# New planned durations and a new model of transfers in a list scheduler that orders every engine's stream

## Chip, cores and metric

One NeuronCore of a Trainium2 chip runs the whole program. The metric is device microseconds from launch to end, as the median of several runs. TensorE is called PE in the profile, VectorE DVE, ScalarE ACT, GpSimd POOL; SyncE (SP) issues the transfers. All times here are in us unless marked ns.

## What is computed

Attention that keeps the 32 largest scores of each row, and behind it two feed-forward networks (FFNs) on the same 2304 tokens:

```
scores = scale * q @ k.T                       # 4 batches, 8 heads, 576 positions, 64 wide
kth    = partition(scores, -32)[..., -32]      # the 32nd largest of each row
attn   = softmax(where(scores >= kth, scores, -1e9))
x      = (attn @ v) as (2304 tokens, 512)
h      = x @ w_in;  g = max(0.01 * h, h);  y = g @ w_out               # 512 -> 2048 -> 512
z      = max(y @ w1, y @ w2, y @ w3) @ w_out2                          # 512 -> 768 -> 512
```

The FFNs' weights come as 64-bit floats. The results must be close to 32-bit precision, so a matrix product is made of three 16-bit ones (high part by high, high by low, low by high).

## The kernel before

**Attention** runs in 72 steps, numbered from 0 in the order of the program; a step is 128 query rows of one pair of heads, or 64 rows of two pairs. A step's work goes through all engines in turn:

- SP loads K (`kt`) and Q (`qt`, L397 to L408) from the prepared copy `dqk` in memory; PE multiplies them (L693) into the score tile `s`, of which there is one; ACT copies it to `S` (L698), twice for each step (halves 0 and 1 of `S`; there are three buffers `S`).
- DVE searches the 32 largest: four times `MAX8` (L708) and three times a replace (L710: `MATCH_VALUE_LOAD`, then `MATCH_REPLACE8`) for each half.
- POOL makes the biases `nt` and `nb` (L718 to L727); ACT masks (L732), takes the exponential (L735) and rounds to 16 bits (L738, `phl`); POOL subtracts for the low part (L740).
- SP transposes `phl` to `pt` (L743), PE multiplies with V (L769 to L771, called the weighting product here), DVE takes the reciprocal of the sums (L776, L777), ACT scales (L779) and rounds (L785), POOL subtracts (L787), and once a block is full SP transposes it to `xu` (L805), the input of the FFN.

**Preparation.** For each batch and pair of heads `prep_qk` loads Q and K into `raw` (two buffers; for batch 0 into space of `wo`), squares them (L340), finds a power of two (L325 on DVE, L332 and L334 on POOL), scales (L351), splits (L352, L353) and writes both parts to `dqk` (L380). `v_stats` (L426) and `prep_v` (L440) do the like for V, with the same buffers `raw`. The FFN's weights are repacked from 64 bits by DVE (L487, L490, L493), their norms taken (ACT L512, PE L518, DVE L523), and scaled and split as above (`w<-in_w_in` at L476 and so on).

**The FFNs** run in ten units of 128 to 256 tokens. PE's work in them is groups of three products (L811, L812, L813). Between them stand ACT (L859, L866), POOL (L872) and DVE (L956), and at the change from the first network to the second a chain through L909, L912 and L914. Results go to memory at L994.

**The order.** Nothing of the order is written by hand. Each call of `op` makes a node with its engine, a planned duration, what it reads and writes, and a priority: `TP(i)` for step `i`, less 100 for scores and weighting product, and a running clock for the FFN units. `Plan.run` (L123) is a list scheduler. It goes through planned time; on each engine it takes, of the nodes that may start, the one of lowest priority value, adds the planned duration, and frees buffers at the planned ends. For SP's transfers it keeps one planned path. The planned start times, sorted, give the order in which the instructions are written, and so each engine's fixed order on the chip. On the chip an engine waits for the semaphores of its next instruction and does nothing else meanwhile; planned times themselves appear nowhere in the program.

## Time and profile before

| | us |
|---|---|
| median of 3 runs (1081.46, 1085.2, 1085.3) | 1085.2 |
| the profiled execution, in all | 1083.86 |
| its span, first to last instruction | 1081.9 |
| PE busy | 901.3 |
| DVE busy | 876.3 |
| ACT busy | 840.9 |
| POOL busy | 600.0 |
| mean granted clock of PE, as a share of 2.4 GHz | 0.935 |

The 2.0 us between span and whole lie outside of what the trace shows. Shares over the whole span say little here, since the program has stages: first weights and attention alone, then attention and FFN side by side, at the end the FFN alone. So the profile is read by stage, and where two engines hand work to each other, by the two instructions concerned. A busy time on PE is not PE at its peak, because products overlap.

### The profile page before, as it was taken

The numbers are of one execution on the slowest core, as the hardware profiler recorded it, in microseconds if no ns is written. First come the engines' busy times: TensorE is split into PE (matmuls) and PEld (weight loads), VectorE is DVE, ScalarE is ACT, GpSimd is POOL, SyncE is SP. The second block draws the span as 40 slices with busy tenths as digits, with TensorE's granted clock in tenths as the row PEclk, the third lists the DMA queues.
The fourth block names the chain that finished last, engine by engine and source line by source line (L and its number), as shares of the span: only waits on it lengthen the run. The fifth ranks groups of instructions, "written<-read, shape, count | busy, mean of one in ns | idle before, by whom it ended". The sixth has DMA issues, their size and how long they took to land.

```text
span 1081.9 us, 27366 instructions
## 1 busy us (share of the span) xinstructions
PE 901.3 (83%) x10292; PEld 794.4 (73%) x10292; DVE 876.3 (81%) x2010; ACT 840.9 (78%) x1769; POOL 600.0 (55%) x1110
## 2 busy tenths in 40 slices
PE   2334334498998998998999899999989999999998
PEld 2122223387998887887888688878878897889998
DVE  3999999998999999999649899989599999910101
ACT  7866888898799888788979777888997788664242
POOL 4554766686467655566655545666774555443131
PEclk9995556689999999999999999999999999999999
DMA  7878628647555333354753333554834433220000
GB/s 258 284 195 259 222 52 227 199 102 150 105 124 118 91 80 87 77 125 128 177 127 85 81 70 96 135 122 105 186 83 87 92 72 84 64 56 7 21 2 16
DMA packets 268516, 125.78 MB, mean 116 GB/s; under 512 B 237408, under 2 KB 255328, under 8 KB 266336
## 3 DMA queue, kind: packets, MB, share of 16 engines
q1 hardware_dynamic: 268384, 124.04, 45.7%
q8 instruction: 81, 1.33, 0.5%
q14 instruction: 51, 0.42, 0.1%
HBM read 62.65 MB, written 14.16 MB: 71 GB/s over the span
## 4 chain that ended last, share of the span: by engine, by line
PE 49%; DVE 19%; DMA 11%; ACT 10%; POOL 5%; issue 4%; SPq 2%; POOLq 0%; ACTq 0%; DVEq 0%
PE h L811 8%; PE h L812 8%; PE h L813 8%; DMA pt<-phl 6%; DVE m L708 5%; PE acc L811 5%; PE acc L812 5%; PE acc L813 5%; DVE w L710 5%; PE s L693 4%; DVE acc L487 2%; PE h L769 2%; POOL phl L740 2%; DVE w L493 2%; PE h L770 2%
## 5 line engine op out<-in xcount | busy, mean ns | idle before, releaser
L708 DVE MAX8 m<-w 128x8 f32<-128x576 f32 x432 | 309.1, 747 | 0.2
L740 POOL TENSOR_TENSOR phl<-pp,phl 128x576 f16<-128x576 f32 x144 | 183.8, 1281 | 110.2 <-ACT phl L738 105.4
L872 POOL TENSOR_TENSOR f16t<-k,f16t 128x256 f16<-128x256 f32 (+2 forms) x220 | 136.7, 623 | 190.0 <-ACT f16t L866 165.6
L710 DVE MATCH_REPLACE8 w<-m,w 128x576 f32<-128x576 f32 x288 | 212.2, 742 | 0.0
L811 PE MATMUL h<-k,w 128*128 128x256 f16 (+2 forms) x720 | 187.2, 264 | 9.4 <-ACT k L912 4.8
L812 PE MATMUL h<-k,w 128*128 128x256 f16 (+2 forms) x720 | 187.2, 264 | 4.4 <-POOL k L914 4.1
L813 PE MATMUL h<-k,w 128*128 128x256 f16 (+2 forms) x720 | 187.4, 265 | 0.0
L812 PE MATMUL acc<-f16t,wo 128*128 128x256 f16 (+2 forms) x640 | 165.7, 263 | 3.6 <-POOL f16t L872 3.6
L811 PE MATMUL acc<-f16t,wo 128*128 128x256 f16 (+2 forms) x640 | 165.8, 263 | 0.4 <-ACT f16t L866 0.4
L813 PE MATMUL acc<-f16t,wo 128*128 128x256 f16 (+2 forms) x640 | 165.7, 263 | 0.0
L811 PE MATMUL h<-xu,wi 128*128 128x256 f16 (+1 forms) x576 | 154.5, 268 | 1.3 <-DVE colt L325 0.8
L812 PE MATMUL h<-xu,wi 128*128 128x256 f16 (+1 forms) x576 | 154.5, 268 | 0.0
L813 PE MATMUL h<-xu,wi 128*128 128x256 f16 (+1 forms) x576 | 154.5, 268 | 0.0
L693 PE MATMUL s<-kt,qt 128*128 128x288 f16 (+5 forms) x800 | 107.8, 283 | 50.3 <-ACT S L698 35.8
L866 ACT ACTIVATE f16t<-k 128x256 f16<-128x256 f32 (+2 forms) x220 | 86.1, 393 | 54.2 <-DVE k L956 51.7
L735 ACT ACTIVATE pp<-pp,nb,colt 128x576 f32<-128x576 f32 x144 | 123.1, 862 | 0.2
L708 DVE MAX8 m<-S 128x8 f32<-128x576 f32 x144 | 103.1, 744 | 19.5 <-ACT S L698 19.3
L732 ACT ACTIVATE pp<-S,nt 128x576 f32<-128x576 f32 x144 | 107.8, 768 | 13.0 <-POOL phl L740 8.6
L859 ACT ACTIVATE k<-h,colt 128x256 f32<-128x256 f32 (+2 forms) x160 | 72.0, 452 | 58.5 <-PE h L813 57.5
L693 PEld LDWEIGHTS <-qt 128*128 128x128 f16 (+1 forms) x800 | 62.8, 107 | 68.9 <-issue 43.8
L812 PEld LDWEIGHTS <-w 128*128 128x128 f16 x960 | 94.3, 98 | 19.6 <-issue 11.0
L698 ACT ACTIVATE S<-s 128x576 f32<-128x576 f32 x144 | 92.6, 643 | 18.6 <-PE s L693 17.7
(132 smaller groups left out, 2520.4 us busy)
## 6 DMA issues: line engine op xcount, KB each, us to landing
rw<-in_w SPq DMA_DIRECT2D x18, 512.0 KB, 4.8
w<-in_w_in SPq DMA_DIRECT2D x8, 1024.0 KB, 8.1
w<-in_w_out SPq DMA_DIRECT2D x8, 1024.0 KB, 5.0
raw<-in_qk SPq DMA_DIRECT2D x24, 288.0 KB, 3.3
dqk<-hl SPq DMA_DIRECT2D x48, 144.0 KB, 2.5
kt<-dqk SPq DMA_DIRECT2D x16, 288.0 KB, 3.1
qt<-dqk SPq DMA_DIRECT2D x144, 32.0 KB, 2.2
raw<-in_v SPq DMA_DIRECT2D x12, 352.0 KB, 3.3
```

The source lines that it names most:

```text
L693: T.matmul(p()[osl, h, o:o + w], q()[:, hh, st, :n], k()[:, hh, kc:kc + w], start=st == 0, stop=st == 1, skip_group_check=True)
L698: op(ACT, act(S, True), lambda t=t, p=p: A.activation(t().rearrange("p (a s) -> p a s", a=2), p()[:, :, :288], AF.Copy), r=[p], w=[(Sp, j) ...
L708: op(DVE, dve(S) * 1.03, lambda mc=mc, src=src: V.max(mc(), src()), r=rd, w=[(m, j, 0, r)], pr=pd)
L710: op(DVE, dve(S) * 1.03 + 0.06, lambda mc=mc, src=src, j=j: V.match_replace(out=wp()[:, j], in_to_replace=mc(), in_values=src(), imm_value ...
L732: op(ACT, act(S, aps=1), lambda j=j: A.activation(pp()[:, j], Sb[j](), AF.Prelu, bias=nt()[:, j:j + 1], alpha=STEEP), r=[(Sp, j), nt], w=[ ...
L735: op(ACT, act(S, aps=2), lambda j=j, es=es: A.activation(pp()[:, j], pp()[:, j], AF.Exp, bias=nb()[:, j:j + 1], scale=es), r=[(nb, j), ((" ...
L740: op(POOL, pool(S), lambda j=j: G.tensor_tensor(phl()[:, 1, j], pp()[:, j], phl()[:, 0, j], op=ALU.subtract), r=[(pp, j), (phl, 0, j)], w= ...
L811: T.matmul(out, wt(0), xt(0), start=first, stop=False, skip_group_check=True)
L812: T.matmul(out, wt(0), xt(1), start=False, stop=False, skip_group_check=True)
L813: T.matmul(out, wt(1), xt(0), start=False, stop=last, skip_group_check=True)
L866: op(ACT, act(N), lambda: A.activation(hl()[:, 0, :N], g()[:, 0, :N], AF.Copy), r=[(g, 0)], w=[(hl, 0)], pr=pr)
L872: op(POOL, pool(N) + 0.044, lambda: G.tensor_tensor(hl()[:, 1, :N], g()[:, 0, :N], hl()[:, 0, :N], op=ALU.subtract), r=[(g, 0), (hl, 0)], ...
```

## The change

The planned durations of ACT, POOL, DVE's top-k and three transfers change, and the planner's model of transfers does: before, each transfer held the one path for its whole planned time `n.dma`; now it holds it for 0.6 of that, lands after its whole time, and no transfer may be issued before the eighth last one has landed. No instruction, tile or buffer changes.

```diff
+DSH = 0.6
         dma_free = 0.0
+        lanes = [0.0] * 8
...
-                    t, ok = max(n.ready, t0), True
+                    t, ok = max(n.ready, t0, lanes[-8] if e == SP else 0.0), True
...
             if n.eng == SP:
                 st = max(t + 1.1, dma_free)
-                dma_free = st + n.dma
-                end = dma_free + 0.95
+                dma_free = st + DSH * n.dma
+                end = st + n.dma + 0.95
+                lanes.append(end)
...
 def act(n, psum=False, aps=0):
-    return (n * 0.833 + (70 if psum else 120) + 105 * aps) / 1000
+    return (n * 0.833 + (52 if psum else 94) + 93 * aps) / 1000
...
 def pool(n):
-    return (n * 2.13 + 110) / 1000
+    return (n * 1.905 + 142) / 1000
...
-                    op(DVE, dve(S) * 1.03, lambda mc=mc, src=src: V.max(mc(), src()), r=rd, w=[(m, j, 0, r)], pr=pd)
+                    op(DVE, dve(S), lambda mc=mc, src=src: V.max(mc(), src()), r=rd, w=[(m, j, 0, r)], pr=pd)
...
-                    op(DVE, dve(S) * 1.03 + 0.06, lambda mc=mc, src=src, j=j: V.match_replace(
+                    op(DVE, dve(S) + 0.06, lambda mc=mc, src=src, j=j: V.match_replace(
...
-        op(SP, 2.4, lambda: Y.dma_start_transpose(pt().rearrange("p a c q -> p (a c) q"),
+        op(SP, 2.05, lambda: Y.dma_start_transpose(pt().rearrange("p a c q -> p (a c) q"),
...
-            op(PE, 15 * mm(64) * (1 if full else 2) * (COLD if i < NCOLD else 1), avm, r=[pt] + [(vt, x) for x in range(3)], w=[avb, (xs, "a"), (xhl, "a", i)], pr=pa)
+            op(PE, 15 * mm(68) * (1 if full else 2) * (COLD if i < NCOLD else 1), avm, r=[pt] + [(vt, x) for x in range(3)], w=[avb, (xs, "a"), (xhl, "a", i)], pr=pa)
...
-                op(SP, 1.5, lambda u=u, uo=uo, so=so, w=w: Y.dma_start_transpose(
+                op(SP, 1.25, lambda u=u, uo=uo, so=so, w=w: Y.dma_start_transpose(
```

Besides, POOL's `nt` and `nb` are planned 0.05 to 0.1 shorter, and four terms of 0.044 or 0.06 that were added to `pool(n)` are gone. `dma(nbytes)` stays at 255 GB/s, and the latencies between engines stay. In the changed file a line after L126 has a number higher by up to 3 (L698 is L701 there).

What moves is the order on all five engines; after the first instructions hardly a stretch is the same. Three places follow.

**ACT, at the start.** `S` is the score copy of step 0, `s` its product, `w_76` the first weights of `w_in`, `wo` is batch 0's Q and K, `raw` batch 1's. Before, from the 19th instruction on:

```order
L340 ACTIVATE junk_244,colt<-raw_141 128x576
L352 ACTIVATE wo<-wo 128x576
L512 ACTIVATE junk_254<-w_76 128x512
L352 ACTIVATE wo<-wo 128x576
L351 ACTIVATE w_76<-w_76,colt 128x1024
L352 ACTIVATE wo<-wo 128x576 x2
L352 ACTIVATE wi<-w_76 128x4x256
L512 ACTIVATE junk_280<-w_76 128x512
L698 ACTIVATE S_293<-s_283 128x576
```

Now, from the same place on:

```order
L515 ACTIVATE junk_229<-w_76 128x512
L354 ACTIVATE wo<-wo,colt 128x576
L515 ACTIVATE junk_242<-w_76 128x512
L355 ACTIVATE wo<-wo 128x576
L701 ACTIVATE S_263<-s_245 128x576
L354 ACTIVATE wo<-wo,colt 128x576
L515 ACTIVATE junk_280<-w_76 128x512
L355 ACTIVATE wo<-wo 128x576
L701 ACTIVATE S_263<-s_272 128x576
L354 ACTIVATE w_76<-w_76,colt 128x1024
```

The copy went ahead of the scaling of the first weights and of batch 1's square.

**ACT, at step 33**, where batch 2's preparation falls: `pp` and `phl` are the step's weights, `f16t`, `k` and `acc` are of the FFN unit 3, `hl` and `raw` of batch 2. Before:

```order
L732 ACTIVATE pp_7713<-S_7206,nt_7661 128x576
L866 ACTIVATE f16t_7728<-k_1154_7690 128x256
L351 ACTIVATE raw_7131<-raw_7131,colt 128x576
L351 ACTIVATE raw_7268<-raw_7268,colt 128x576
L352 ACTIVATE hl_7754<-raw_7131 128x576
L859 ACTIVATE k_1161_7764<-h_7720,colt 128x256
L732 ACTIVATE pp_7713<-S_7206,nt_7661 128x576
L866 ACTIVATE f16t_7779<-k_1161_7764 128x256
L698 ACTIVATE S_7799<-s_7663 128x576
L735 ACTIVATE pp_7713<-pp_7713,nb_7673,colt 128x576 x2
L909 ACTIVATE k_1167_7838<-acc_6951,colt 128x256 x2
```

(the step's two `phl` follow twelve and fourteen rows after the last `L735`). Now:

```order
L735 ACTIVATE pp_7612<-S_7100,nt_7604 128x576 x2
L869 ACTIVATE f16t_7633<-k_1141_7597 128x256
L701 ACTIVATE S_7639<-s_7558 128x576
L862 ACTIVATE k_1150_7645<-h_7620,colt 128x256
L738 ACTIVATE pp_7612<-pp_7612,nb_7607,colt 128x576 x2
L869 ACTIVATE f16t_7697<-k_1150_7645 128x256
L741 ACTIVATE phl_7699<-pp_7612 128x576 x2
```

Here the step's six operations stand together, ahead of batch 2's preparation and of the change of networks; beside them stand the 12th and 13th tiles of the FFN unit (of 16) where before there were the 15th and 16th. Counted on PE, 795 groups of three FFN products stand ahead of this step's weighting product, where 829 did.

**SP, where batch 2's last pair of heads is loaded** (`kt`, `qt` out of `dqk_3`), which step 37 waits for. Before:

```order
L380 DMA dqk_3_90<-hl_8575 64x2x576 x2
L440 DMA raw_8643<-in_v 128x704
L743 DMA_TRANSPOSE pt_8652<-phl_8541 128x18x128
L994 DMA out_T<-k_1279_8667 128x256 x2
L994 DMA out_T<-k_1280_8678 128x256 x2
L805 DMA_TRANSPOSE xu_8729<-xhl_8311 128x8x64
L405 DMA qt_8754<-dqk_3_90 128x2x64
```

Now:

```order
L383 DMA dqk_3_90<-hl_8591 64x2x576 x2
L443 DMA raw_8642<-in_v 128x704
L443 DMA raw_8693<-in_v 128x704
L408 DMA qt_8696<-dqk_3_90 128x2x64
L411 DMA qt_8696<-dqk_3_90 64x2x64 x2
L997 DMA out_T<-k_1285_8705 128x256 x2
```

The load of Q passed two transposes and the output stores, and a further load of V came ahead of it.

## Rows read from the trace of the kernel before

**Rows 1.** By stage: length, PE, PEld, DVE, ACT, POOL, clock, DMA share, GB/s.

```profile
30.00:200.00 170.00, 67.31 (x628) 47.66 (x626) 169.92 (x366) 134.71 (x223) 99.42 (x147) 0.67 0.69 210
200.00:320.00 120.00, 102.49 (x1360) 97.01 (x1359) 112.30 (x271) 106.98 (x251) 76.29 (x150) 0.90 0.57 129
320.00:520.00 200.00, 187.30 (x2295) 165.68 (x2292) 194.83 (x454) 172.73 (x376) 122.22 (x232) 1.00 0.44 103
...
960.00:1081.00 121.00, 116.12 (x1263) 108.90 (x1260) 11.78 (x31) 43.00 (x114) 31.73 (x61) 1.00 0.05 15
```

**Rows 2.** Timeline: start, length, instruction; last searches and weighting products of three steps.

```profile
438.87 0.76 DVE L708 MAX8 m<-w 128x8 f32<-128x576 f32 x1
452.80 0.19 PE L769 MATMUL h<-vt,pt 128*128 128x65 f16 x1
...
671.44 0.74 DVE L708 MAX8 m<-w 128x8 f32<-128x576 f32 x1
688.61 0.19 PE L769 MATMUL h<-vt,pt 128*128 128x65 f16 x1
...
925.81 1.41 DVE L708 MAX8 m<-w 128x8 f32<-128x576 f32 x2
938.83 0.19 PE L769 MATMUL h<-vt,pt 128*128 128x65 f16 x1
```

**Rows 3.** Timeline of DVE: searches and replaces without a pause between them.

```profile
34.45 1.41 DVE L708 MAX8 m<-w 128x8 f32<-128x576 f32 x2
35.78 0.07 DVE L710 MATCH_VALUE_LOAD w<-m,w 128x8 f32 x1
...
36.50 0.08 DVE L710 MATCH_VALUE_LOAD w<-m,w 128x8 f32 x1
```

**Rows 4.** DVE where step 0 begins (brackets: idle before, ended by).

```profile
29.69 0.42 DVE L523 TENSOR_REDUCE colt<-h 128x1 f32<-128x256 f32 x1 [5.15 <-PE h L518]
30.03 0.75 DVE L708 MAX8 m<-S 128x8 f32<-128x576 f32 x1
```

**Rows 5.** Timelines of PE and ACT before step 0's score copy.

```profile
25.22 1.17 PE L693 MATMUL s<-kt,qt 128*128 128x288 f16 x4
...
25.27 1.13 ACT L351 ACTIVATE w<-w,colt 128x1024 f32<-128x1024 f32 x1
...
27.46 1.04 ACT L352 ACTIVATE wi<-w 128x1024 f16<-128x1024 f32 x1
28.40 0.61 ACT L512 ACTIVATE junk<-w 128x512 bf16<-128x512 f32 x1
28.92 0.62 ACT L698 ACTIVATE S<-s 128x576 f32<-128x576 f32 x1
```

**Rows 6.** Timeline of SP's issues at the start.

```profile
10.01 1.08 SPq L369 DMA_DIRECT2D raw<-in_qk  x2
```

**Rows 7.** Timeline of PE: first FFN product, and the pace of its groups.

```profile
196.75 0.36 PE L811 MATMUL h<-xu,wi 128*128 128x192 f16 x1
...
452.14 0.27 PE L811 MATMUL h<-xu,wi 128*128 128x256 f16 x1
...
452.47 0.27 PE L811 MATMUL h<-xu,wi 128*128 128x256 f16 x1
```

**Rows 8.** Timelines of SP and DVE where step 37's second half begins.

```profile
544.69 1.24 SPq L380 DMA_DIRECT2D dqk<-hl  x2
...
553.88 0.57 SPq L405 DMA_DIRECT2D qt<-dqk  x1
...
558.69 0.76 DVE L708 MAX8 m<-S 128x8 f32<-128x576 f32 x1 [12.21 <-ACT S L698]
```

**Rows 9.** Waits of PE from 320 to 1050: total, times, longest.

```profile
PE s L693 <- ACT S L698: 7.8, 7, 2.8
PE h L769 <- DMA pt<-phl: 5.0, 8, 1.1
```

**Rows 10.** All 72 transposes of the weights, issue to landing.

```profile
DMA to landing us min/median/max: 3.9/4.0/7.3
```

More of the change, by code (lines that the diff above doesn't have):

```diff
@@ L717, in attention @@
         c2 = lambda c: m()[:, :, c:c + 1].rearrange("p a o -> p (a o)")
-        op(POOL, 0.3, lambda: G.tensor_scalar(nt(), c2(TOPK - 1), -1.0, None, op0=ALU.mult),
+        op(POOL, 0.2, lambda: G.tensor_scalar(nt(), c2(TOPK - 1), -1.0, None, op0=ALU.mult),
            r=tk(0) + tk(1), w=[nt], pr=pr)
-        op(POOL, 0.25, lambda: G.tensor_tensor(nb(), c2(TOPK - 1), c2(0), op=ALU.subtract),
+        op(POOL, 0.2, lambda: G.tensor_tensor(nb(), c2(TOPK - 1), c2(0), op=ALU.subtract),
            r=tk(0) + tk(1) + [(m, 0, 0, 0), (m, 1, 0, 0)], w=[(nb, 0), (nb, 1)], pr=pr)
         if full:
-            op(POOL, 0.34, lambda: G.tensor_scalar(nb(), nb(), ES[b, hps[0]], LNPS, op0=ALU.mult, op1=ALU.add),
+            op(POOL, 0.28, lambda: G.tensor_scalar(nb(), nb(), ES[b, hps[0]], LNPS, op0=ALU.mult, op1=ALU.add),
                r=[(("es", b, hps[0]), 1)], w=[(nb, 0), (nb, 1)], pr=pr)
@@ L726, in attention @@
             for j in range(2):
-                op(POOL, 0.34, lambda j=j: G.tensor_scalar(nb()[:, j:j + 1], nb()[:, j:j + 1], ES[b, hps[j]], LNPS,
+                op(POOL, 0.28, lambda j=j: G.tensor_scalar(nb()[:, j:j + 1], nb()[:, j:j + 1], ES[b, hps[j]], LNPS,
                                                            op0=ALU.mult, op1=ALU.add),
@@ L786, in attention @@
            w=[(xhl, 0, g0)], pr=pr)
-        op(POOL, pool(64 * nh) + 0.06, lambda: G.tensor_tensor(xo(1), xi(), xo(0), op=ALU.subtract),
+        op(POOL, pool(64 * nh), lambda: G.tensor_tensor(xo(1), xi(), xo(0), op=ALU.subtract),
            r=[(xs, h) for h in range(nh)] + [(xhl, 0, g0)], w=[(xhl, 1, g0)], pr=pr)
@@ L871, in hilo @@
                 return hl
-            op(POOL, pool(N) + 0.044, lambda: G.tensor_tensor(hl()[:, 1, :N], g()[:, 0, :N], hl()[:, 0, :N],
+            op(POOL, pool(N), lambda: G.tensor_tensor(hl()[:, 1, :N], g()[:, 0, :N], hl()[:, 0, :N],
                                                      op=ALU.subtract), r=[(g, 0), (hl, 0)], w=[(hl, 1)], pr=pr)
@@ L913, in ffn @@
                r=[(ff, e)], w=[(yh, e)], pr=pr)
-            op(POOL, pool(N) + 0.044, lambda e=e, f=f: G.tensor_tensor(yl()[:, e, :N], f(), yh()[:, e, :N],
+            op(POOL, pool(N), lambda e=e, f=f: G.tensor_tensor(yl()[:, e, :N], f(), yh()[:, e, :N],
                                                               op=ALU.subtract), r=[(ff, e), (yh, e)], w=[(yl, e)],
```

## The prediction

> **What bounds the kernel now.** I read the busy times by stage first, then the start of each engine's stream, then pairs of instructions in which one engine hands a step to the next, and last the waits.
>
> By stage [rows 1]: from 30 to 200 us VectorE works 169.9 of 170 us and TensorE 67 of 170, at a granted clock of 0.67. From 320 to 520 both are nearly full (VectorE 194.8, TensorE 187.3 of 200). After 960 VectorE is done and TensorE alone runs out the last FFN units, 116 of 121 us. So two engines bound this kernel in turn: VectorE (weight repacking and the top-32) until the first FFN unit runs, then the two together, then TensorE. TensorE's work does not change, so the end moves by what TensorE loses or saves in idle time: by how much earlier its FFN work begins, and by how often it must wait for a step of attention that VectorE has not finished.
>
> Each step ends in a weighting product (L769 to L771). Its shortest way from the last top-k search is seen at step 69: the search ends at 925.81 + 1.41 = 927.2, the product starts at 938.83, 11.6 us [rows 2]. At step 28 the same way takes 13.2 us (439.6 to 452.80), at step 47 16.4 us (672.2 to 688.61). So at step 28 TensorE comes only 1.6 us, and at step 47 4.8 us, after the earliest moment at which VectorE lets it.
>
> **The change, part by part.**
>
> *Prices in the planner.* No instruction is added or taken away; a planned duration is only a number. The old prices stood above the trace: a top-k search was planned at 0.689 us and takes 0.665 (two in 1.33), a replace at 0.749 and takes 0.72 [rows 3]; now 0.669 and 0.729. ScalarE and GpSimd come down alike, TensorE's prices were right and stay. So the old plan gave TensorE more FFN work per step than VectorE's real pace needs, which is cover: TensorE arrives late and seldom waits. The new plan takes the cover away. Whatever happens comes from the order.
>
> *The start.* VectorE idles 5.15 us before 29.69 and begins step 0's search at 30.03 [rows 4]. The step's score copy ran at 28.92 on ScalarE, though its product was over at 25.22 + 1.17 = 26.4 [rows 5]: weight scaling stood before it, an operation at 25.27 (1.13 us long, of which some 0.1 overlaps the next), one of 0.94 (27.46 to 28.40) and one of 0.52 (28.40 to 28.92). In the new order 22 instead of 29 ScalarE instructions stand before the copy: away are these three, one more of 0.52, one of about 0.7 and two of about 0.6, in all 4.4 us. If the product came no earlier, the copy could move by 2.5 us only; but K and Q of step 0 also move up in SP's queue, past two loads of a later batch (1.08 us of issue at 10.01) and three writes [rows 6]. Bounds -2.5 and -4.4, taken -4: VectorE's saturated stretch begins 4 us earlier. The work of batch 1 that made room (its first head pair) goes behind step 5, where ScalarE and GpSimd have it to do besides the first FFN unit; no one needs it before step 18.
>
> *The first FFN unit.* It starts at 196.75 [rows 7] and waits for step 5. On VectorE 306 instead of 316 instructions stand ahead of that step's reciprocal: six searches (0.665) and three replaces (0.72) fewer and one repacking operation (0.6) more, 5.6 us less; with the earlier start -9.6 us for TensorE's FFN work. Bounds: 0 if ScalarE, which has 13 instructions fewer there too, holds it up, and -10.
>
> *Does TensorE keep it?* VectorE's own order past step 8 is the same to about 1 us at each step. Its pace is therefore the old one, moved by the start (-4) and by what of its 7.7 us of idle time between 200 and 320 [rows 1] goes; it waits there for TensorE, which now comes earlier: between 0 and -7.7, taken -3. So VectorE runs at -7. Before the weighting product of step 28 stand 18 groups of three FFN products fewer than before (664 for 682), at 0.33 us each (452.14 to 452.47) [rows 7] 5.9 us less cover. The product can start at -7 - 1.6 = -8.6; for the same FFN work TensorE is then at -8.6 + 5.9 = -2.7. Of the 9.6 us won it has stood idle through 7.
>
> *Batch 2.* VectorE waits 12.21 us for step 37's second score copy (558.69) [rows 8]. Its Q load was issued at 553.88, behind four output stores and an x transpose. In the new order stores and transpose stand elsewhere, but a third V load stands ahead of it, which needs a free input buffer. The score parts were written by 545.9, so the load could go about 6 us earlier; with what the preparation itself gains or loses (its VectorE steps stand 4 to 7 us later in a stream that runs 7 earlier) the restart moves by -10 to +1, taken -7.
>
> *Steps 37 to 53.* Here the new order places least FFN work: 34 groups fewer before step 47 (1178 for 1212), 11.2 us. The product can start at -7 - 4.8 = -11.8, so TensorE stands at -11.8 + 11.2 = -0.6 for the same work: nearly all is lost. At step 69 the two orders agree again (1788 and 1787 groups), and what follows is TensorE's alone.
>
> *Other waits.* From 320 to 1050 TensorE waited 7.8 us for score copies and 5.0 for transposed weights [rows 9]. Truer prices could take them away or, with less cover, double them: -8 to +13, taken -1.5.
>
> *Transfers.* The new plan lets each transfer hold the path for 0.6 of its time, so 255 GB/s become 425. In the trace the path moved 210 GB/s while its engines were busy 0.69 of the time (30 to 200 us) [rows 1], some 304 GB/s at full share: the truth lies between the two plans. A transpose of the weights takes 3.9 to 7.3 us to land, median 4.0 [rows 10]; alone it is planned at 4.15. So only those that stand beside other transfers land later than planned. The Trainium skill (DMA: Bandwidth & Descriptors, Rules for kernel authors and Issuing engines are not separate DMA queues) says that DMAs in flight together run on the same 16 engines and only interleave, which speaks against planning 0.6; the trace agrees in part, 304 for 425 GB/s. By that rule every such landing would come late and the slower rival below would be the case.
>
> **The sum.** -0.6 - 1.5 = -2.1 us on the profiled execution's span of 1081.9 us, 1079.8, and with the 2.0 us outside of it (1083.86 in all) 1081.8. The median of the three runs lies 1.3 us above the profiled one, less than the runs differ among themselves; I say 1082.
>
> **Rivals.** *The early start is kept* (faster): if VectorE restarts at step 37 by 12 us or more earlier, or runs at -10 already by step 28, the product of step 47 is no limit and TensorE keeps its -9.6: 1083.9 - 9.6 = 1074; with half of the 12.8 us of waits gone too, 1068. For it: VectorE waited for TensorE in 200 to 320, and the order of step 33 on ScalarE no longer lets the next batch's preparation stand within the step. Against it: batch 2's own chain on VectorE is later in the stream.
>
> *Batch 2 is late* (slower): the place is the Q load of step 37. If the third V load waits for its buffer, or the preparation (4 to 7 us later in the stream) sets the pace, VectorE restarts at 0 or later. TensorE has then 11.2 us less to do before step 47 and the product may start at -4.8: +6.4, and with the same at batch 3 (whose third head pair stands 11 us later in VectorE's stream against a shift of 7) up to +10: 1090 to 1094. It decides from a restart of about -1 on. Transposes that land later than planned add to this, at 0.3 us for each of some 26 steps that lost cover, 8 us if none is hidden.
>
> *Nothing moves*: both orders are paced by VectorE and the FFN's end alike; 1084. This lies within the forecast's own band.
>
> **How the numbers follow.** Forecast (within about 4 us of 1082) 0.42, with nothing moves in it; early start kept 0.36; batch 2 late 0.22. A measurement can tell about 0.5%, 5.4 us, from no change: faster 0.36, same 0.42, slower 0.22. The range leaves out a tenth on either side: down to 1070, between the two prices of the faster rival, up to 1093, near the upper price of the slower one.
>
> **What would show it.** Step 0's search should start at 25 to 27.5 us and the first FFN product at 186 to 190; if they don't, the first two steps are wrong. TensorE should show waits for transposed weights about steps 26 to 29 and 44 to 47 that it did not have; if it has none there, the gain was kept and the time is near 1074. VectorE's restart at step 37 should lie near 552; near 558 or later means the slower rival. The forecast is wrong if the waits of the FFN's own chain (ScalarE and GpSimd to TensorE) grow or vanish by more than some 5 us, since I took them as nearly unchanged.

## The result

The changed kernel takes 1099.8 us (median of 1100.82, 1098.78, 1095.24 and 1101.26) where the kernel before takes 1085.25 beside it: a ratio of 1.0134, 95% interval 1.0095 to 1.0173. It is slower by some 14.5 us, outside the range of the prediction (1070 to 1093). The profiled execution took 1100.82 us, of which the span is 1098.7 (1083.86 and 1081.9 before); the two traces differ by 16.7 us of span. Line numbers of the kernel after are up to three higher (L708 is now L711, L769 is L772, L811 is L814).

By stage, as in [rows 1] (length, PE, PEld, DVE, ACT, POOL, granted clock, DMA share, GB/s), the kernel after:

```profile
30.00:200.00 170.00, 65.62 (x610) 47.01 (x609) 160.43 (x343) 132.67 (x219) 93.84 (x140) 0.65 0.66 203
200.00:320.00 120.00, 99.52 (x1245) 92.83 (x1243) 108.54 (x262) 103.84 (x240) 73.77 (x142) 0.88 0.54 127
320.00:520.00 200.00, 182.43 (x2234) 161.34 (x2231) 187.46 (x435) 161.94 (x355) 114.85 (x216) 0.97 0.45 92
...
978.00:1098.00 120.00, 114.77 (x1249) 107.65 (x1246) 11.77 (x30) 41.99 (x111) 30.93 (x60) 1.00 0.04 11
```

VectorE has lost its full stretch: 160.4 of 170 us where it was 169.9, and it stays lower in the next two stages. TensorE does 5 us less between 320 and 520. The last stage is alike.

**The start.** VectorE where step 0 begins, and the first FFN product, which answer to [rows 4] and [rows 7]:

```profile
23.12 0.42 DVE L526 TENSOR_REDUCE colt<-h 128x1 f32<-128x256 f32 x1 [1.44 <-PE h L521]
...
23.90 0.76 DVE L711 MAX8 m<-S 128x8 f32<-128x576 f32 x1 [0.17 <-ACT S L701]
...
190.07 0.34 PE L814 MATMUL h<-xu,wi 128*128 128x192 f16 x1 [2.29 <-DMA xu<-xhl]
```

The search starts 6.1 us earlier (23.90 for 30.03) and the first FFN product 6.7 (190.07 for 196.75). Both are gone soon after: TensorE begins FFN group 100 (of 2240) 3.8 us later than before and group 400 10.7 later. What VectorE waited for between 40 and 240 us (total, times, longest), in the kernel after:

```profile
DVE colt L534 <- PE h L314: 3.3, 2, 2.7
DVE colt L526 <- PE h L521: 3.2, 3, 2.1
DVE h L490 <- DMA rw<-in_w: 3.2, 6, 1.3
DVE r L779 <- PE h L774: 2.0, 3, 0.9
DVE colt L433 <- PE h L314: 1.3, 1, 1.3
```

and in the kernel before:

```profile
DVE colt L531 <- PE h L311: 1.5, 1, 1.5
DVE colt L325 <- PE h L311: 0.2, 1, 0.2
```

13.0 us against 1.7: for TensorE's sums of squares and weighting products, and for weights still on their way.

**The steps.** Last searches and weighting products of steps 28, 47 and 69, against [rows 2]:

```profile
449.93 1.41 DVE L711 MAX8 m<-w 128x8 f32<-128x576 f32 x2
465.60 0.20 PE L772 MATMUL h<-vt,pt 128*128 128x65 f16 x1 [0.70 <-DMA pt<-phl]
...
683.97 1.41 DVE L711 MAX8 m<-w 128x8 f32<-128x576 f32 x2
698.89 0.19 PE L772 MATMUL h<-vt,pt 128*128 128x65 f16 x1
...
943.42 0.75 DVE L711 MAX8 m<-w 128x8 f32<-128x576 f32 x1
955.53 0.19 PE L772 MATMUL h<-vt,pt 128*128 128x65 f16 x1
```

The products come 12.8, 10.3 and 16.7 us later than before. TensorE's waits for transposed weights in steps 19 to 35, the kernel after (320 to 540 us), then the kernel before (310 to 515 us):

```profile
PE h L772 <- DMA pt<-phl: 4.7, 6, 1.1
```

```profile
PE h L769 <- DMA pt<-phl: 0.7, 3, 0.4
```

So there the cover is missing, as the prediction had it: at steps 27 to 31 TensorE stands before a weighting product for 0.5 to 1.0 us each time.

**TensorE's own pace.** From its first FFN product to the end of the span, with the columns of [rows 1], the kernel before, then the kernel after:

```profile
196.75:1081.93 885.18, 828.29 (x9676) 743.55 (x9674) 698.75 (x1626) 685.63 (x1510) 487.89 (x910) 0.98 0.41 94
```

```profile
190.07:1098.67 908.60, 842.17 (x9690) 753.42 (x9690) 707.52 (x1649) 689.79 (x1524) 492.72 (x918) 0.97 0.42 93
```

This stretch is 23.4 us longer after. TensorE's idle time makes 9.5 us of that (66.4 for 56.9), and its busy time 13.9, though it does the same products. They follow each other more slowly where the granted clock is at its lower level. In the kernel after TensorE waits three times between 331.5 and 335.1 us, for 1.2, 0.5 and 0.9 us; behind that the record gives 0.50 (1.2 GHz) between 335.6 and 340.9, and 1.00 (2.4 GHz) between 341.2 and 346. A group of three products of 128 columns takes 0.32 us in the first stretch and 0.16 in the second (from one L814 to the next):

```profile
336.06 0.31 PE L814 MATMUL h<-k,w 128*128 128x128 f16 x1
...
336.38 0.31 PE L814 MATMUL h<-k,w 128*128 128x128 f16 x1
...
344.98 0.22 PE L814 MATMUL h<-k,w 128*128 128x128 f16 x1
...
345.14 0.22 PE L814 MATMUL h<-k,w 128*128 128x128 f16 x1
```

By the record TensorE has 44 us of its work after the first FFN product at the lower level, where it had 23 before. At half the pace that is some 11 of the 13.9 us, an estimate from these rows. No run changes the clock alone, so what it is worth in the end is not shown.

**The restarts.** Batch 2's last pair of heads (step 37) and batch 3's third (step 56), in the kernel after. The products `h<-colt,ones` are `prep_qk`'s sums of squares on TensorE, from which the scaling, the store of `dqk`, the loads of K and Q and the scores follow:

```profile
560.40 0.28 PE L314 MATMUL h<-colt,ones 128*128 128x1 f32 x2
...
570.91 0.38 SPq L408 DMA_DIRECT2D qt<-dqk  x1
...
576.09 0.76 DVE L711 MAX8 m<-S 128x8 f32<-128x576 f32 x1 [6.66 <-ACT S L701]
...
766.13 0.50 PE L314 MATMUL h<-colt,ones 128*128 128x1 f32 x4
...
780.84 0.16 DVE L328 TENSOR_SCALAR colt<-h 128x1 int32<-128x1 int32 x1 [10.44 <-PE h L314]
787.95 0.16 DVE L328 TENSOR_SCALAR colt<-h 128x1 int32<-128x1 int32 x1 [6.95 <-PE h L314]
791.15 0.76 DVE L711 MAX8 m<-S 128x8 f32<-128x576 f32 x1 [3.05 <-ACT S L701]
```

Before, the same pair of events for step 56:

```profile
745.51 0.95 PE L311 MATMUL h<-colt,ones 128*128 128x1 f32 x8
...
770.97 0.76 DVE L708 MAX8 m<-S 128x8 f32<-128x576 f32 x1 [2.43 <-ACT S L698]
```

Step 37's second half restarts at 576.09 for 558.69 [rows 8], 17.4 later; step 56 at 791.15 for 770.97, 20.2 later. The search of step 56 follows its sum of squares by 25.0 us after and by 25.5 before. And that sum stands, on TensorE, at one place of the FFN's work: behind group 1340 in both orders; the sums of batch 2's second pair stand behind group 780 in both (those of the third and fourth pair behind 826 to 870). Why they stand there: a preparation has the due time of its step less `LB` = 60 and the priority number that follows from it; FFN units with lower numbers go first, whenever their inputs are there. (The sums of batch 2's second pair have the number 364.4; FFN group 779 has 363.5 and group 780 has 364.7.) So VectorE's next batch hangs on TensorE's progress through FFN groups. By group 1340 TensorE is 20.2 us late (766.5 for 746.3); 3.4 of it are won back behind.

### The profile page after: what moved, and what is told of

The parts are those of the page before. It is cut to its first block, busy times and chain, and to the rows that moved or that the text cites. A ratio compares the mean times of both kernels' runs of the same rounds, so it can differ in the third digit from the quotient of the medians.

```text
span 1098.7 us, 27397 instructions
## 1 busy us (share of the span) xinstructions
PE 911.6 (83%) x10292; PEld 801.6 (73%) x10292; DVE 876.8 (80%) x2010; ACT 837.7 (76%) x1769; POOL 598.3 (54%) x1110
## 4 chain that ended last, share of the span: by engine, by line
PE 45%; DVE 9%; ACT 9%; DMA 7%; POOL 5%; issue 5%; SPq 1%; POOLq 0%; ACTq 0%; DVEq 0%
PE h L815 8%; PE h L814 8%; PE h L816 8%; DMA pt<-phl 5%; PE acc L814 5%; PE acc L815 5%; PE acc L816 5%; DVE m L711 4%; DVE w L713 4%; PE s L696 3%; POOL phl L743 2%; PE h L772 2%; PE h L773 1%; PE h L774 1%; ACT pp L735 1%
## 5 line engine op out<-in xcount | busy, mean ns | idle before, releaser
L711 DVE MAX8 m<-w 128x8 f32<-128x576 f32 x432 | 309.7, 747 | 0.3
L743 POOL TENSOR_TENSOR phl<-pp,phl 128x576 f16<-128x576 f32 x144 | 183.6, 1281 | 99.6 <-ACT phl L741 96.5
L814 PE MATMUL h<-k,w 128*128 128x256 f16 (+2 forms) x720 | 188.2, 265 | 12.7 <-ACT k L915 6.7
L814 PE MATMUL acc<-f16t,wo 128*128 128x256 f16 (+2 forms) x640 | 166.9, 264 | 0.5 <-ACT k L912 0.5
L814 PE MATMUL h<-xu,wi 128*128 128x256 f16 (+1 forms) x576 | 156.3, 271 | 7.1 <-DMA xu<-xhl 4.3
L815 PE MATMUL h<-xu,wi 128*128 128x256 f16 (+1 forms) x576 | 156.5, 272 | 0.0
L816 PE MATMUL h<-xu,wi 128*128 128x256 f16 (+1 forms) x576 | 156.4, 272 | 0.0
L735 ACT ACTIVATE pp<-S,nt 128x576 f32<-128x576 f32 x144 | 107.5, 769 | 32.7 <-POOL nt L721 29.3
L711 DVE MAX8 m<-S 128x8 f32<-128x576 f32 x144 | 102.7, 745 | 16.8 <-ACT S L701 16.6
L772 PE MATMUL h<-vt,pt 128*128 128x65 f16 (+1 forms) x800 | 90.6, 201 | 27.5 <-DMA pt<-phl 19.4
L815 PEld LDWEIGHTS <-w 128*128 128x128 f16 x960 | 94.9, 99 | 23.8 <-issue 15.6
L701 ACT ACTIVATE S<-s 128x576 f32<-128x576 f32 x144 | 92.4, 642 | 24.7 <-PE s L696 24.2
```

The costliest lines, as they stand in the source:

```text
L701: op(ACT, act(S, True), lambda t=t, p=p: A.activation(t().rearrange("p (a s) -> p a s", a=2), p()[:, :, :288], AF.Copy), r=[p], w=[(Sp, j) ...
L711: op(DVE, dve(S), lambda mc=mc, src=src: V.max(mc(), src()), r=rd, w=[(m, j, 0, r)], pr=pd)
L735: op(ACT, act(S, aps=1), lambda j=j: A.activation(pp()[:, j], Sb[j](), AF.Prelu, bias=nt()[:, j:j + 1], alpha=STEEP), r=[(Sp, j), nt], w=[ ...
L743: op(POOL, pool(S), lambda j=j: G.tensor_tensor(phl()[:, 1, j], pp()[:, j], phl()[:, 0, j], op=ALU.subtract), r=[(pp, j), (phl, 0, j)], w= ...
L772: T.matmul(o, hc, vh, start=c == 0, stop=False, skip_group_check=True)
L814: T.matmul(out, wt(0), xt(0), start=first, stop=False, skip_group_check=True)
```

## Experiments

All labels below are kernels of their own; the ratio is to runs of the kernel before on the same chip. The columns after the ratio are from each profiled execution: when TensorE does the sums of batch 2's second pair, when it begins FFN group 1340, when step 56's search starts, the span, and what lies between group 1340 and the end.

| kernel | median | ratio [95%] | sums | group 1340 | step 56 | span | rest |
|---|---|---|---|---|---|---|---|
| before | 1085.2 | | 494.0 | 746.3 | 771.0 | 1081.9 | 335.6 |
| after | 1099.8 | 1.0134 [1.0095, 1.0173] | 517.7 | 766.5 | 791.2 | 1098.7 | 332.2 |
| old_start | 1099.65 | 1.0128 [1.0098, 1.0158] | 503.5 | 758.0 | 782.6 | 1092.3 | 334.3 |
| new_start | 1102.04 | 1.0149 [1.0117, 1.0182] | 514.4 | 768.3 | 793.2 | 1100.7 | 332.4 |
| transfers_only | 1086.05 | 1.0013 [1.0000, 1.0026] | 507.5 | 752.9 | 776.5 | 1085.5 | 332.6 |
| durations_only | 1095.43 | 1.0109 [1.0081, 1.0137] | 498.6 | 752.8 | 777.4 | 1091.0 | 338.2 |
| search_only | 1097.08 | 1.0104 [1.0044, 1.0164] | 503.3 | 762.4 | 788.0 | 1097.7 | 335.3 |
| search_old | 1099.74 | 1.0135 [1.0094, 1.0176] | 508.6 | 761.5 | 786.2 | 1096.1 | 334.5 |
| late_prep_before | 1094.70 | 1.0100 [1.0069, 1.0131] | 529.7 | 759.4 | 804.1 | 1093.8 | 334.4 |
| early_prep_before | 1071.00 | 0.9868 [0.9826, 0.9910] | 448.9 | 741.6 | 737.0 | 1067.8 | 326.2 |
| earlier_prep_before | 1069.46 | 0.9866 [0.9837, 0.9896] | 441.6 | 744.5 | 739.0 | 1067.3 | 322.8 |
| early_prep_after | 1087.23 | 1.0023 [0.9995, 1.0051] | 457.9 | 754.0 | 746.2 | 1082.4 | 328.4 |
| early_prep_transfers | 1077.94 | 0.9940 [0.9919, 0.9961] | 455.5 | 747.6 | 740.8 | 1075.7 | 328.1 |
| early_prep_durations | 1070.05 | 0.9871 [0.9845, 0.9898] | 451.6 | 743.2 | 736.3 | 1069.9 | 326.7 |
| early_b2 | 1091.99 | 1.0063 [1.0040, 1.0086] | 457.7 | 757.5 | 783.0 | 1088.6 | 331.1 |
| early_b3 | 1098.59 | 1.0138 [1.0097, 1.0179] | 513.1 | 767.1 | 769.1 | 1093.2 | 326.1 |
| share_only | 1088.91 | 1.0037 [1.0020, 1.0055] | 500.0 | 753.2 | 777.5 | 1086.6 | 333.4 |
| lanes_only | 1085.86 | 1.0016 [0.9998, 1.0035] | 500.9 | 748.2 | 770.8 | 1081.3 | 333.1 |

The last five columns are of one execution, which need not be the median one: old_start's took 1094.36 us (median 1099.65), early_b3's 1095.00 (1098.59), early_prep_after's 1084.23 (1087.23). Differences of a few us between rows are therefore not to be read. In the kernels whose preparation is not moved the rest is 332 to 338 us, so most of what is lost is lost by group 1340.

### Which half of the program, which half of the change

First theory: the loss is the start's, where VectorE is no longer full. old_start gives every duration both values and takes the old one for what is planned before 240 us (new_start the other way round):

```diff
+    return np.array([o, w])
...
+            dur = n.dur if isinstance(n.dur, float) else float(n.dur[1 if t >= TSW else 0])
...
-                dma_free = st + DSH * n.dma
+                dma_free = st + n.dma * (0.6 if (t >= TSW) == True else 1.0)
```

> Each planned duration has both values; an instruction planned before 240 us takes the old one (and the old transfer model), a later one the new. So the order up to 240 us planned is word for word that of the kernel before, and what follows is planned as in the kernel after. Theory 'start': what is lost is lost where VectorE is no longer full between 40 and 240 us (186.9 us busy of 200 after, 198.1 before). Then VectorE is busy about 198 us of 40 to 240 here, and the time is that of before or lower, 1078 to 1086. Rival 'cover and batches': the new prices lose the time behind the start (later restarts of VectorE at batches 2 and 3, less FFN work per step): then this kernel has before's start and still 1093 to 1100.

> The mirror image: new prices and transfer model up to 240 us planned, old ones after. Theory 'start': VectorE is busy only about 187 us of 40 to 240, and the time is 1095 to 1101. Rival 'cover and batches': the loss of the start is made up behind it, as the old order has slack; time 1083 to 1089.

old_start in 40 to 240 us, PE, PEld and DVE first:

```profile
40.00:240.00 200.00, 90.85 (x902) 71.31 (x902) 198.15 (x440) 165.90 (x299) 124.29 (x198) 0.89 0.63 191
```

VectorE is as full as before (198.15 us; the kernel after has 186.86) and the time is that of the kernel after. The theory of the start falls: with the rest of the new order behind it, the old start buys nothing. No search up to step 35 is more than 0.8 us later than in before, but the orders behind 240 us place 26 FFN groups fewer ahead of step 29 and 27 fewer ahead of step 32; TensorE comes 9.4 us late to the sums of batch 2, and from there the loss runs on. TensorE's busy time behind the first FFN product is that of before (+0.8 us) and its idle time 10.3 us longer, so a loss of 10 us, as in this execution, needs no lower clock. new_start is no better, with 22 groups fewer at the same steps. Its time lies just above the 1095 to 1101 that the theory of the start forecast, and the reason given there fails too, since old_start lost as well.

transfers_only is the kernel before with the new transfer model, durations_only the kernel after with the old one:

```diff
-DSH = 0.6
+DSH = 1.0
...
-                    t, ok = max(n.ready, t0, lanes[-8] if e == SP else 0.0), True
+                    t, ok = max(n.ready, t0), True
```

> The kernel before with only the transfer model of the kernel after (0.6 of a transfer's time on the path, at most eight under way); all durations old. If the start's loss comes from transfers that land later than planned (weight loads that VectorE then waits for), VectorE is busy about 187 us of 40 to 240 here too and the time is 1092 to 1100. If it comes from the shorter durations, the time is 1080 to 1087.

> The kernel after with the old transfer model (each transfer holds the path for its whole time, no limit on the number under way): only the durations are new. By the transfers' theory VectorE is full again from 40 to 240 (about 198 us) and the time is 1078 to 1087; by the durations' theory (cover taken away, batches later) it stays at 1093 to 1100.

transfers_only in 40 to 240 us:

```profile
40.00:240.00 200.00, 89.03 (x814) 68.00 (x815) 187.57 (x420) 162.75 (x283) 126.12 (x195) 0.93 0.62 185
```

The transfer model alone empties VectorE's start (187.57) and costs nothing in the end, 1.0013: TensorE is 13.5 us late at batch 2's sums, but 6.6 at group 1340 and 3.6 at the end. Its order has 22 FFN groups fewer ahead of step 29, but at most 6 fewer ahead of steps 36 to 53 (the kernel after has up to 48 fewer there). durations_only has VectorE full (198.76 us) and loses 1.0109. So the durations alone lose without the start, and the transfer model alone loses the start without losing time. Where the loss arises is less clear than that: in these two executions TensorE begins group 1340 equally late (6.5 and 6.6 us), and durations_only loses another 2.6 us behind it, where transfers_only wins 3.0.

### Is it the FFN work that the plan puts ahead of the steps?

search_only changes one price of the kernel before, search_old puts the same price back into the kernel after:

```diff
-                    op(DVE, dve(S) * 1.03, lambda mc=mc, src=src: V.max(mc(), src()), r=rd, w=[(m, j, 0, r)], pr=pd)
+                    op(DVE, dve(S), lambda mc=mc, src=src: V.max(mc(), src()), r=rd, w=[(m, j, 0, r)], pr=pd)
...
-                    op(DVE, dve(S) * 1.03 + 0.06, lambda mc=mc, src=src, j=j: V.match_replace(
+                    op(DVE, dve(S) + 0.06, lambda mc=mc, src=src, j=j: V.match_replace(
```

> The kernel before with one price changed: the top-k searches and replaces without the factor 1.03. Its order has 31 FFN groups fewer than before ahead of the weighting products of steps 29 to 32 and 34 to 38 fewer ahead of those of steps 50 to 53; the preparation of batch 2's second head pair and of batch 3's third stand on TensorE behind FFN groups 780 and 1340, as in all six kernels so far. Theory 'FFN debt': fewer FFN groups per step let TensorE reach groups 780 and 1340 later, with them the preparation, and VectorE waits longer at steps 37 and 56: time 1091 to 1099, VectorE's first search of step 56 at 780 us or later (770.9 before). Rival: the loss comes from ScalarE's and GpSimd's prices; then 1080 to 1087.

> The kernel after with only the old price of searches and replaces (factor 1.03) put back. Its order has 4 to 11 FFN groups fewer than before ahead of steps 20 to 38 (after: 20 to 27 fewer at steps 28 to 32), and up to 30 fewer ahead of steps 47 to 53 (after 48). Theory 'FFN debt' : TensorE reaches group 780 some 8 to 12 us earlier than in the kernel after, the restarts follow, time 1084 to 1092. Rival, ScalarE's, GpSimd's and the transfers' prices do it: 1096 to 1102, as after.

search_only is the clearest case: VectorE runs 4 to 8 us *ahead* of before from step 14 to step 33, yet TensorE, with 31 FFN groups fewer ahead of steps 29 to 32, comes 9.3 us late to batch 2's sums and 16.1 late to group 1340; step 56 starts at 788.0. 0.02 us less for each planned search and replace cost 1%. (Ahead of steps 50 to 53 its order has 22 to 34 groups fewer, not 34 to 38.) But search_old missed: at most 14 groups fewer than before up to step 38, 13 to 19 more at steps 24 to 27, and still 1.0135. TensorE did come to batch 2's sums 9.1 us earlier than in the kernel after, as forecast, and the time did not fall. There VectorE is 10 to 13 us late at step 18; that TensorE lost by this is likely, but not shown. So the search price is enough for a loss of 1% and not needed for one. What the kernels that lose 1% or more with the preparation in its place share is that TensorE comes late to group 780 (by 5 to 24 us) and to group 1340 (by 6.5 to 22). This alone is not enough either: transfers_only comes 13.5 and 6.6 us late and loses 0.1%.

### Does the preparation's place decide?

One number moves the preparation of batches 2 and 3 (48, 96 and 120 in late_prep_before, early_prep_before and earlier_prep_before):

```diff
-    LB = 60
+    LB = 96
```

> The kernel before with the preparation of batches 2 and 3 due 12 units (one step) later. On TensorE the products of batch 2's last three pairs stand behind 796 to 904 FFN groups (780 to 868 before), those of batch 3's third behind 1374 to 1389 (1340). If the preparation's place among the FFN groups sets the restarts, 36 more groups at 0.33 us delay step 37 by 12 us and some 34 to 49 more delay step 56 by 11 to 16 us: time 1093 to 1108. If the restarts were slack: 1081 to 1087.

> The kernel before with one number changed: the due time of the preparation of batches 2 and 3 lies 36 units (three steps) earlier. On TensorE the statistics products of batch 2's last three head pairs stand behind 668 to 745 FFN groups (780 to 868 before), those of batch 3's third behind 1248 to 1268 (1340 before). Theory 'FFN debt': the place of the preparation in TensorE's FFN sequence is what makes VectorE wait at steps 37 and 56 (27 us idle from 490 to 600 and 14 us from 745 to 800); with it moved, most of this goes, and the time is 1060 to 1075. Rival: the end is set by TensorE's own FFN work, VectorE's waits are slack: 1080 to 1087.

> The kernel before with the preparation due 60 units (five steps) earlier: products behind 664 to 749 and 1188 FFN groups (668 to 745 and 1248 to 1268 with 36 units, which took 1071 us). With 36 units VectorE ran 22 to 30 us ahead of before from step 39 on and TensorE 14 us, so VectorE should no longer be the limit: within 4 us of 1071. If VectorE still was, 1060 to 1066.

VectorE around the two restarts, first before, then early_prep_before:

```profile
490.00:600.00 110.00, 104.84 (x1220) 90.73 (x1218) 82.59 (x192) 93.21 (x203) 69.25 (x134) 1.00 0.54 127
745.00:800.00 55.00, 53.10 (x568) 46.26 (x566) 40.99 (x97) 51.70 (x112) 40.42 (x73) 1.00 0.64 148
```

```profile
490.00:600.00 110.00, 107.17 (x1299) 93.19 (x1297) 104.26 (x239) 96.95 (x208) 67.28 (x125) 1.00 0.54 125
745.00:800.00 55.00, 53.36 (x575) 47.09 (x574) 46.91 (x106) 50.43 (x113) 34.21 (x53) 1.00 0.56 126
```

VectorE's idle time falls from 27.4 to 5.7 us at the first and from 14.0 to 8.1 at the second, and the kernel takes 1071 us: faster than both kernels, by 1.3% and 2.6%. Later preparation costs 1.0%, and earlier still brings no more, probably because TensorE then runs out its own work: behind group 1340 it needs 323 to 328 us wherever batch 3's preparation is early, and 331 to 338 elsewhere.

> The kernel after with the same number changed (preparation due three steps earlier): products behind 668 to 746 and 1268 to 1271 FFN groups. Theory 'FFN debt': VectorE's waits at the two restarts go (28 us idle from 500 to 620, 26 us from 765 to 822 in the kernel after); time 1062 to 1080, and the distance to the kernel before with the same number, now 14.5 us, shrinks to that of the start, 0 to 10 us. Rival (end set by TensorE, or the start's lost 11 us decide): 1093 to 1100.

> durations_only with the preparation 36 units earlier. If the 16 us between early_prep_before and early_prep_after come from the durations, 1080 to 1088; if from the transfer plan's start, 1066 to 1075 (VectorE is full from 40 to 240 us in durations_only, 198.8 us).

> transfers_only with the preparation 36 units earlier, as in early_prep_before (1071) and early_prep_after (1087). With the restarts out of the way TensorE's own lost time decides. If the 16 us between those two come from the start, which the transfer plan alone changes (VectorE 187.6 us busy of 40 to 240), this one takes 1078 to 1088; if from the durations (FFN groups taken from steps 28 to 53), 1066 to 1075.

The same number in the three kernels with new prices. With the new durations alone the whole loss is gone (1070.05, as with the old ones; 1095.43 without it): their loss went through the preparation. In the kernel after it is not gone. early_prep_after takes 1087.23 us, above its 1062 to 1080, and its distance to early_prep_before is 16 us, where I forecast 0 to 10 and where the two kernels without the earlier preparation lie 14.5 apart. So the old place of the preparation costs both kernels about as much (14 and 13 us), and does not by itself explain the loss of the whole change. I had expected those 16 us to be the transfers' or the durations': alone these give +7 and -1, so about 10 us come from the two together, and I have no run that says how. The traces say where. Against early_prep_before, TensorE in early_prep_after is 8.6 us late at FFN group 600, 9.1 at group 780, 14.7 at group 900 and 14.6 at the end; in early_prep_transfers it is 6.6 late at group 600 and 7.9 at the end. With the long waits at the restarts out of the way, what the new start loses does reach the end. One more caution: the earlier preparation lies among steps 22 to 35 and makes them longer, so the plan puts more FFN work there (early_prep_before has 21 groups more than before ahead of step 29, early_prep_after 5 more where the kernel after has 20 fewer). These runs move both, the sums and the cover.

early_b2 and early_b3 are the kernel after with the one or the other preparation moved:

```diff
-        t = TP(i) - (-hp * (hp < 2) if b == 0 else LB1 if b == 1 else LB)
+        t = TP(i) - (-hp * (hp < 2) if b == 0 else LB1 if b == 1 else 96 if b == 2 else LB)
```

> The kernel after with the preparation of batch 2 alone due 36 units earlier: its products behind 668 to 746 FFN groups, those of batch 3's third pair behind 1344 as in after (1340). If only the last restart counts, step 56 still starts 25 us after TensorE's group 1340 (766 us in after) and the time stays at 1096 to 1101. If the restart at step 37 counts too, VectorE runs some 30 us earlier from step 39 on, TensorE waits less for it and reaches group 1340 by 752 to 760: 1085 to 1094.

> The kernel after with the preparation of batch 3 alone due 36 units earlier: products of its third pair behind 1260 FFN groups (1340), those of batch 2 as in after. If the last restart sets the end, VectorE's step 56 comes up to 20 us earlier than the 791 us of after and the time is 1083 to 1092. If what was lost by the restart at step 37 stays lost on TensorE, 1093 to 1100.

Of the 12.6 us that both together bring, batch 2 carries most. Moving its preparation brings TensorE to group 1340 9.0 us earlier and the time down by 7.8; step 56 still follows. Moving batch 3's brings VectorE's step 56 from 791.2 to 769.1 and the time down by 1.2 only: TensorE is at group 1340 as late as in the kernel after (767.1). I had half expected the last restart to set the end; it does not. What TensorE has lost by then stays lost.

### The two halves of the transfer model

> The kernel before with 0.6 of a transfer's time on the path and no limit on the number under way. If the share is what lets loads land later than planned, VectorE is busy 185 to 190 us of 40 to 240 (198.1 before, 187.6 in transfers_only). Time by step 56's rule (product behind group 1340, plus 25, plus 310) between 1083 and 1092.

> The kernel before with at most eight transfers under way and each still holding the path for its whole time. If the share is the cause at the start, VectorE stays full from 40 to 240 (197 to 199 us). The order changes all through, though no price does, so this run also shows what a mere reordering moves: 1081 to 1092, by the place at which TensorE reaches group 1340 (8 FFN groups or fewer off before's).

```diff
 # share_only
+                dma_free = st + DSH * n.dma
+                end = st + n.dma + 0.95
...
 # lanes_only
+                    t, ok = max(n.ready, t0, lanes[-8] if e == SP else 0.0), True
...
+                lanes.append(end)
```

lanes_only in 40 to 240 us:

```profile
40.00:240.00 200.00, 91.05 (x903) 71.51 (x903) 197.85 (x440) 164.56 (x294) 122.03 (x189) 0.73 0.66 186
```

The limit of eight leaves VectorE full and the time alike (1.0016), though its order differs from before's almost from the first instructions: a new order need not cost anything. It has 19 FFN groups fewer than before ahead of step 29, but at most 8 fewer ahead of steps 36 to 53. The share of 0.6 takes part of VectorE's start (192.31 us busy, where I had expected 185 to 190) and costs 0.4%. The Trainium skill (DMA: Bandwidth & Descriptors, Issuing engines are not separate DMA queues) says that transfers run on the same 16 DMA engines and interleave there, whichever engine started them. The traces agree in part: with the share of 0.6 the weight loads `rw` out of `in_w` land after 5.6 us in the median in the kernel after and 5.3 in transfers_only (4.8 before), but after 4.3 in share_only. VectorE waits 3.2 us for them in the kernel after.

## Why the prediction was wrong

- **Start of step 0** (-4, up to -4.4): right in kind, -6.1, so beyond its bound. The step's product itself was over at 22.65 us, for 26.4 before.
- **First FFN product** (-9.6): -6.7, just outside of 186 to 190. It did not matter, since unit 0's later groups waited.
- ***Does TensorE keep it?*** is the step that failed. I let VectorE run at -7 by step 28, because it was saturated before [rows 1] and the streams are alike past step 8. Measured: its last search of step 28 ends 11.7 us *later*. Saturation was a property of the old order: in the new one TensorE's sums and the weights come when the plan does not expect it, 13.0 us of waits for 1.7. Search by search VectorE is 6.1 us early at step 0, 7.1 late by 228 us and 10 to 12 late from 340 to 430. So of the 18.7 us between term and measurement 11.1 are there by 228 us (+7.1 for the -4 of the start). Another part is the idle time between 200 and 320, of which I took off 3 us: it rose from 7.7 to 11.5.
- **TensorE's work** is the second premise that failed. I wrote that it does not change, and counted idle time alone. The products are the same, but from the first FFN product on TensorE is busy for 13.9 us more and idle for 9.5 more; the sum had no term for a lower clock behind the waits.
- **The arithmetic of cover** held. With the measured shift of the product, step 28 gives 12.8 + 5.9 = 18.7 (TensorE is 20.7 late at group 682), step 47 gives 10.3 + 11.2 = 21.5 (23.8 at group 1212). The waits for transposed weights came at steps 27 to 31 as said; about step 45 there were none.
- **Restart of batch 2** (-7, bounds -10 to +1): +17.4. I looked at the last link, the Q load in SP's queue [rows 8], and at VectorE's stream. The queue did give what I read there: from the pair's last sums of squares to the search it took 24.1 us before (534.6 to 558.69) and 15.7 after (560.40 to 576.09), 8.4 less, for the 6 or so expected. But the sums themselves came 25.8 us later, since they stand behind 868 and 870 FFN groups on TensorE: -8.4 + 25.8 = +17.4. The cover that I priced as a loss of FFN work for TensorE was therefore also a delay of VectorE's next batch, a term that the sum did not have.
- **Other waits** (-1.5): about right. Between 320 and 1050 us TensorE waits 5.2 us for score copies and 4.9 for transposed weights, 2.7 less than before. The waits of the FFN's products for ScalarE and GpSimd are 19.1 us over the whole span for 16.8, inside of the 5 us that I named as a mark of error. The units' first products waited 7.1 us instead of 1.3, but 4.3 of this for `xu`, which comes from attention.
- **Prices**: I wrote that TensorE's prices stay, and counted three transfers with new prices. The change also plans the weighting product longer (`mm(68)` for `mm(64)`, 0.025 us a step), and the transfers are two (L743, L805). No run has these alone.
- **The slower rival** had place and sign: restart at 0 or later, batch 3 worse. Its 1090 to 1094 was too low, because it priced a restart at 0, and from that +6.4 at step 47; the restart came at +17.4, and TensorE stood at +23.8 there. It deserved more than 0.22: the trace of before shows the sum of squares at 745.51 behind FFN work, with its inputs squared by 732.5.

What stays open: how transfers and durations together cost some 10 us more than their sum once the preparation is early, why search_old loses in spite of its cover, and how much of the loss is the lower clock's. That the preparation's place among the FFN groups sets VectorE's restarts is shown by moving it; that this is the whole of the change's loss is not.

## To carry over

Where one engine's fixed order mixes work that feeds another engine with work that only fills time, "cover" and "delay" are the same instructions: follow a long wait back past its last link to the place in the filling engine's stream. After repricing a list scheduler, compare its planned times with the trace: the old plan starts its last instruction at 1080.5 us for a span of 1081.9, the new one at 1057.0 for 1098.7, and it is 14 us ahead of the chip by step 9 already. Yet the prices of ScalarE, GpSimd and VectorE came nearer to the trace: GpSimd's subtractions of 576 columns follow each other every 1.240 us, planned at 1.337 before and 1.239 now. Truer prices did not help here, where the waits that they no longer pad were not planned; one due time was worth more (1071 us) than all of them. And a wait on TensorE is to be counted twice, as idle time and as products that run at the lower clock behind it, where the record shows one.

## Unexpected on the hardware

The record of the granted clock can lack its first part, and what is missing is shown as full speed. Between 120 and 160 us the record grants TensorE the upper level in old_start and the lower one in before:

```profile
120.00:160.00 40.00, 14.42 (x137) 10.25 (x137) 40.00 (x89) 37.18 (x53) 29.26 (x41) 1.00 0.33 98
```

```profile
120.00:160.00 40.00, 13.30 (x133) 9.66 (x132) 40.00 (x91) 37.95 (x54) 30.28 (x41) 0.50 0.28 90
```

But four score products of 288 columns take as long in one as in the other. The first row is old_start's, the second that of before:

```profile
146.82 1.12 PE L701 MATMUL s<-kt,qt 128*128 128x288 f16 x4 [0.99 <-ACT S L706]
```

```profile
148.36 1.12 PE L693 MATMUL s<-kt,qt 128*128 128x288 f16 x4 [0.99 <-ACT S L698]
...
333.17 0.65 PE L693 MATMUL s<-kt,qt 128*128 128x288 f16 x4
```

The last row is where before's record gives 1.00, and there the four products take 0.65 us. So by their pace TensorE was at the lower level in old_start as well. Its record has no entry before 165.8 us, that of before none before 77.5 (where the same four products take 1.17 us [rows 5]), so the 0.67 of [rows 1] is too high. Nor does the mean clock go with the time: 13 runs of the kernel before beside old_start had 0.927 to 0.988 at 1081.19 to 1086.02 us, among them 1085.03 at 0.979 and 1082.02 at 0.932. A gap at the start would explain such a spread; that it does in those 13 is not shown. Where the record does have entries, from the first FFN product on, the pace of the products goes with it.
